# Weight loads on ScalarE's queue, tokens in pairs, and the layer norm's epsilon on GpSimd in a four-layer attention kernel

## The chip, the cores and the metric

The kernel runs on one core of a Trainium2 chip. The core has TensorE (PE in the profile: matmuls, PEld: its weight loads), VectorE (DVE), ScalarE (ACT), GpSimd (POOL) and SyncE (SP), which here only issues DMAs. Each engine works through its own list of instructions in order, and the lists meet at semaphores. The metric is the device time of one execution in microseconds. A profiled execution gives the span and the trace of every instruction.

## The reference

One sequence of 2048 tokens of width 512 in bfloat16 goes through four layers, A, B, A, B, each behind a layer norm and with a residual:

```
def _layernorm(x, axis=-1, eps=1e-5):
    m = jnp.mean(x, axis=axis, keepdims=True)
    v = jnp.var(x, axis=axis, keepdims=True)
    return (x - m) / jnp.sqrt(v + eps)

# A: 32 query heads of 16, one key and one value head
q = (x @ wq) in 32 heads;  k = x @ wk;  v = x @ wv
p = softmax(q k^T * 16 ** -0.5);  out = (p v) @ wo

# B: linear attention, 32 heads of 16
phi(t) = where(t > 0, t + 1, exp(t)) + 1e-6
kv = phi(k)^T v;  z = sum of phi(k);  out = (phi(q) kv / (phi(q) z + 1e-6)) @ wo

x = x + A(_layernorm(x)); x = x + B(_layernorm(x))
x = x + A(_layernorm(x)); x = x + B(_layernorm(x))
```

Both A layers use the same weights, and both B layers.

## The kernel before

**Tiles.** The tokens are 16 tiles of 128 (`x_sb`, resident in SBUF). An A layer first normalises each tile, transposes it, and projects queries (`QT`), keys (`KM`, with a masked copy each for two halves of the heads) and values (`V`). The scores are 2048 blocks of 128 keys by 512 (128 tokens of four heads), by QK matmuls of line 841. A block is made into weights in one of two ways:

- ScalarE takes two or three blocks at once with one exponential out of PSUM (line 1016, tile `PT`).
- VectorE builds an approximate exponential from the bits of an integer (line 1103, tile `FB`), and makes shifted copies of four such blocks together (line 1145, SBUF to SBUF); all versions, weighted by `VW`, go into the value product.

The value product is line 895. VectorE takes blocks only when the keys of all 16 tiles are there.

**Layer norm** (`ln_tile`, lines 676 to 719). For each tile: statistics (`bn_stats`, line 685) and aggregate (line 686) on VectorE, variance plus epsilon (`ve`, line 687) on VectorE, the power -0.5 (`rs`, line 689) on GpSimd, and the normalised tile `xn` (line 692) on VectorE. Then a transpose: in the first layer on PE for tiles 0 to 3 (line 712, with a copy out of PSUM at line 603) and by a DMA from SP for tiles 4 to 15 (line 617). While an A layer's scores still run, finished tiles already pass through the layer norm of the next layer.

**What sets the order.** Nothing is ordered by hand. `Planner` plays the kernel through with a duration and a latency that the code gives each operation, chooses by priority among those that are ready, and, where an operation may run on ACT or DVE (`flex`), by which is free. The resulting lists per engine are what is emitted, with semaphore waits from the dependences. So a changed duration or engine anywhere can redraw the order everywhere. Where PE would stand still, the planner gives it filling matmuls without use (line 827 before and between the layers, line 940 within an A layer).

**The start.** All loads are issued by SP through `dma` (line 540), in order of their priority: tiles 0 to 3 singly, then wk, wv, wq, then tiles 4 to 15 in three blocks of four tiles. The late weights (wo, wqkv, the second wo) follow when all keys of the first layer are planned. POOL runs some thirty small memsets and selects (lines 563 to 595: dummies' operands, identities, masks, `kmask`, the ones column of `va`), DVE eight little ones of `kmask` (line 575). ACT loads its table of functions as its first instruction (line 1674), warms it up with an exponential of one column (line 596), and makes `wkr`, wk repeated eight times, with four copies (line 581). In the first layer, `a_tile` lets no tile but the first enter the layer norm before the first tile's power is done.

Of the kernel before, what the change touches and what calls it, by code (L numbers as in the profile page):

```python
# [10 lines left out]
ALU = mybir.AluOpType  # L11
# [4 lines left out]
P = 128  # L16
# [19 lines left out]
class Planner:  # L36
# [256 lines left out]
    def finalize(self):  # L293
# [15 lines left out]
        dmas = [o for o in self.order[SP] if o.isdma]  # L309
# [103 lines left out]
AHEAD = 20  # L413
CHT = 19
# [6 lines left out]
def bass_interleave_layers__grouped_kv_mqa__linear_attn_block__prompt_kernel(  # L421
# [117 lines left out]
    def dma(dst, src, writes, prio, lat):  # L539
        return op({SP: (0.07, lambda e: e.dma_start(dst, src))}, writes=writes, prio=prio, lat=lat, dma=True)  # L540

    for t in range(4):
        dma(x_sb[:, t, :], xv[:, t, :], [("x", t)], 0.1 * t, 2.5 + 0.5 * t)
    dma(wk[:], A_wk.rearrange("(ft f) c -> f ft c", f=P), ["wk"], 1.0, 4.0)
    dma(wv[:], A_wv.rearrange("(ft f) c -> f ft c", f=P), ["wv"], 1.1, 4.2)
    dma(wq[:], A_wq.rearrange("(ft f) c -> f ft c", f=P), ["wq"], 1.2, 5.5)
    for b in range(1, 4):
        dma(x_sb[:, 4 * b:4 * b + 4, :], xv[:, 4 * b:4 * b + 4, :], [("x", t) for t in range(4 * b, 4 * b + 4)], 2.0 + 0.1 * b, 6.0 + 1.5 * b)
    def late():
        yield ("flag", ("K", 0, T - 1))  # L550
        dma(wo[:], A_wo.rearrange("(g r) c -> r g c", r=P), ["wo"], 3.0, 12.0)
        dma(wqkv[:], B_wqkv.rearrange("(ft f) c -> f ft c", f=P), ["wqkv"], 3.1, 15.0)
        dma(wo2[:], B_wo.rearrange("(g r) c -> r g c", r=P), ["wo2"], 3.2, 16.0)
# [6 lines left out]
    def pool_op(fn, writes, reads=(), dur=0.2, prio=0.0):  # L560
        return op({PO: (dur, fn)}, reads=reads, writes=writes, prio=prio)
# [9 lines left out]
    pool_op(lambda e: e.memset(kmask[:, 0:1], 0.0), ["kmask"], dur=0.1)  # L571
    pool_op(lambda e: e.memset(kmask[:, 1:2], KSC), ["kmask"], dur=0.1)
    for j in range(4):
        for r, v in ((0, KSC), (1, 0.0)):
            op({DV: (0.1, lambda e, j=j, r=r, v=v: e.memset(kmask[32 * j:32 * j + 16, r:r + 1], v))}, writes=["kmask"], prio=0.0)
# [4 lines left out]
    for ft in range(FT):  # L580
        op({AC: (0.17, lambda e, ft=ft: e.copy(
            wkr[:, ft, :].rearrange("p (r d) -> p r d", r=8),
            wk[:, ft, :].unsqueeze(1).to_broadcast([P, 8, DH])))}, reads=["wk"], writes=["wkr"], prio=0.5)
    for i in range(NSH):
# [9 lines left out]
    pool_op(lambda e: e.memset(va[:].rearrange("p t (h c) -> p (t h) c", c=17)[:, :, DH:DH + 1], 1.0),  # L594
            [("va", i) for i in range(8)], dur=2.3, prio=2.6)
    op({AC: (1.6, lambda e: e.activation(warm[:], warm[:], ACTF.Exp))}, writes=["warm"], prio=0.0)
# [19 lines left out]
    def dmat(dst, src, reads, writes, prio):  # L616
        return op({SP: (0.1, lambda e: e.dma_start(dst, src, transpose=True))}, reads=reads, writes=writes, prio=prio, lat=DTL, dma=True)
# [61 lines left out]
    def ln_tile(t, prio, far=False, crit=False):  # L679
# [3 lines left out]
        else:  # L683
# [3 lines left out]
        op({DV: (0.07, lambda e: e.tensor_scalar(out=ve[:, t:t + 1], in0=mv[:, t, 1:2], scalar1=1e-5, scalar2=None, op0=ALU.add))},  # L687
           reads=[("mv", t)], writes=[("ve", t)], prio=prio, lat=0.16)
# [32 lines left out]
    def a_tile(L, t, prio):  # L721
        yield ("flag", ("x", L - 1, t))
        if L == 0 and t:
            yield ("sleep", 0.0)
            yield from until(("rs", 0))
        cr = t in MCRIT[L - 1] if L else False
# [946 lines left out]
    def scalar(e):  # L1673
        e.add_instruction(mybir.InstLoadActFuncSet(name=nc.get_next_instruction_name(), engine=mybir.EngineType.Activation, act_func_set_id=LNEXP))
        pl.emit(AC, e)

    with nc.Block() as block:
# [3 lines left out]
        block.scalar(lambda e: scalar(e))  # L1681
# [29 lines left out]
```

## Time and profile before

| what | value |
|---|---|
| runs | 1515.29, 1515.67, 1517.45 us; median 1515.67 |
| profiled execution: time, span | 1518.41 us, 1516.5 us |
| busy PE, DVE, ACT, POOL | 1460.4, 1437.6, 1474.5, 72.3 us |
| granted PE clock, mean | 0.999 |
| first exponential of scores (ACT) | 15.02 us |
| first block on DVE (line 1103) | 43.48 us |
| tile 0, wk, wv, wq issued by SP at | 0.80, 2.66, 3.14, 3.69 us |
| `ve` on DVE, `rs` on POOL (64 each, mean) | 143 ns, 817 ns |

Busy time is the sum of an engine's instructions without overlaps; a group's mean is of one instruction's own duration, and neighbours on DVE and ACT overlap, so that the step from one start to the next is shorter than the duration. "Idle before" names what released an engine from a wait. The landing of a DMA is the time at which its semaphore is complete.

### The profile page before, as it was taken

To read this page: it belongs to the slowest core of one execution; us is meant where nothing else is said; L and a number is where in the kernel's file an instruction comes from. 1 tells how busy PE (TensorE), PEld (TensorE's weight loads), DVE (VectorE), ACT (ScalarE), POOL (GpSimd) and SP (SyncE) were. 2 spreads that over 40 slices of the span, in tenths; PEclk is the share of its full clock that TensorE was granted. 3 is DMA by queue.
4 is the path that set the end of the run, shared out by engine and by line. 5 is a ranking of instruction groups with operands and counts; after the bars stand their busy time and mean duration, and the time that the engine had idled before them with its cause. 6 is when DMAs were issued, how large, how long until landed. Compare 5 with 4: busy or idle time off the path is not lost.

```text
span 1516.5 us, 36545 instructions
## 1 busy us (share of the span) xinstructions
PE 1460.4 (96%) x14867; PEld 527.4 (35%) x14867; DVE 1437.6 (95%) x2701; ACT 1474.5 (97%) x1502; POOL 72.3 (5%) x126
## 2 busy tenths in 40 slices
PE   7999999999999999999999999999999999999999
PEld 4433333332333333323744323333333333333335
DVE  7899999999999999999866899999999999999996
ACT  7999999999999999999699999999999999999996
POOL 4000000000000000000111000000000000000001
PEclk9999999999999999999999999999999999999999
DMA  4200000000000000000001000000000000000001
GB/s 111 73 5 8 9 10 7 8 5 8 8 9 8 5 8 5 1 2 2 2 16 22 9 8 15 9 8 5 8 9 5 9 8 9 5 5 2 2 2 57
DMA packets 46965, 19.15 MB, mean 13 GB/s; under 512 B 40656, under 2 KB 46288, under 8 KB 46800
## 3 DMA queue, kind: packets, MB, share of 16 engines
q1 hardware_dynamic: 46800, 16.82, 4.8%
q8 instruction: 119, 1.95, 0.6%
q14 instruction: 46, 0.38, 0.1%
HBM read 5.28 MB, written 2.10 MB: 5 GB/s over the span
## 4 chain that ended last, share of the span: by engine, by line
issue 79%; PE 11%; ACT 5%; POOL 2%; DVE 1%; DMA 1%; SPq 0%; POOLq 0%; ACTq 0%
ACT PT L1016 5%; PE ps L895 2%; POOL rs L689 2%; PE ps L609 2%; PE ps L841 2%; PE ps L766 1%; PE ps L827 1%; PE ps L940 1%; DMA wq<-in_A_wq_dram 0%; PE ps L1439 0%; PE ps L660 0%; DMA xnT<-xn 0%; PE ps L1187 0%; SPq L540 0%; POOL VW L736 0%
## 5 line engine op out<-in xcount | busy, mean ns | idle before, releaser
L1016 ACT ACTIVATE PT<-ps 128x1024 bf16<-128x1024 f32 (+1 forms) x1338 | 1408.3, 1198 | 6.8 <-PE ps L841 5.1
L1103 DVE TENSOR_SCALAR FB<-ps 128x512 int16<-128x512 f32 x1042 | 685.5, 682 | 8.0 <-PE ps L841 5.8
L841 PE MATMUL ps<-QT,KM 32*128 32x512 bf16 x4096 | 538.4, 385 | 20.8 <-ACT PT L1016 15.4
L895 PE MATMUL ps<-FB,VW 128*32 128x512 bf16 x4168 | 543.6, 385 | 12.9 <-ACT PT L1016 6.4
L1145 DVE TENSOR_SCALAR FB<-FB 128x2048 int16<-128x2048 int16 x786 | 516.2, 677 | 0.7
L895 PE MATMUL ps<-PT,V 128*32 128x512 bf16 x3054 | 488.7, 387 | 7.2 <-ACT PT L1016 5.3
L841 PEld LDWEIGHTS ps<-QT,KM 32*128 32x128 bf16 x4096 | 134.9, 91 | 400.8 <-ACT PT L1016 249.1
L895 PEld LDWEIGHTS ps<-FB,VW 128*32 128x32 bf16 x4168 | 134.3, 94 | 185.8 <-issue 88.4
L940 PE MATMUL ps<-QT,V 128*32 128x512 bf16 (+6 forms) x798 | 197.4, 319 | 1.3 <-DVE QT L1275 0.8
L895 PEld LDWEIGHTS ps<-PT,V 128*32 128x32 bf16 x3054 | 118.8, 93 | 124.1 <-issue 62.5
L689 POOL TENSOR_TENSOR rs<-ve,mhalf 128x1 f32<-128x1 f32 x64 | 52.2, 817 | 1337.7 <-DVE ve L687 1328.5
L940 PEld LDWEIGHTS ps<-QT,V 128*32 128x32 bf16 x798 | 63.8, 95 | 91.1 <-issue 62.4
L609 PE MATMUL ps<-wqkv,xnT 128*128 128x512 bf16 (+1 forms) x272 | 84.8, 373 | 0.5 <-DMA xnT<-xn 0.3
L1187 PE MATMUL ps<-identF,sacc 128*128 128x128 f32 x256 | 47.7, 292 | 2.4 <-DVE sacc L1168 2.0
L1272 ACT ACTIVATE phE<-ps 128x512 bf16<-128x512 f32 (+1 forms) x66 | 41.6, 631 | 7.8 <-PE ps L766 5.8
L1168 DVE COPY sacc<-ps 128x512 f32<-128x512 f32 x64 | 43.7, 682 | 4.9 <-PE ps L895 4.9
L685 DVE BATCH_NORM_STATS2 st<-x_sb 128x6 f32<-128x512 bf16 x60 | 40.7, 679 | 3.2 <-DMA x_sb<-in_A_x_dram 3.0
L609 PE MATMUL ps<-wo,OT 128*128 128x512 bf16 x120 | 42.0, 387 | 0.9 <-DMA OT<-Osb 0.8
L766 PE MATMUL ps<-xnT,wq 128*128 128x128 bf16 x480 | 39.7, 223 | 0.6 <-DMA wq<-in_A_wq_dram 0.5
L766 PE MATMUL ps<-xnT,wqkv 128*128 128x128 bf16 x512 | 39.6, 220 | 0.2
L609 PEld LDWEIGHTS ps<-wqkv,xnT 128*128 128x128 bf16 x272 | 22.2, 97 | 49.4 <-issue 32.8
L1187 PEld LDWEIGHTS ps<-identF,sacc 128*128 128x128 f32 x256 | 27.4, 140 | 25.7 <-issue 14.4
(142 smaller groups left out, 645.0 us busy)
## 6 DMA issues: line engine op xcount, KB each, us to landing
out_dram<-x_sb SPq DMA_DIRECT2D x16, 128.0 KB, 1.7
x_sb<-in_A_x_dram SPq DMA_DIRECT2D x3, 512.0 KB, 6.8
wqkv<-in_B_wqkv_dram SPq DMA_DIRECT2D x1, 1536.0 KB, 8.8
xnT<-xn SPq DMA_TRANSPOSE x48, 2.4
x_sb<-in_A_x_dram SPq DMA_DIRECT2D x4, 128.0 KB, 2.3
wq<-in_A_wq_dram SPq DMA_DIRECT2D x1, 512.0 KB, 4.9
wo<-in_A_wo_dram SPq DMA_DIRECT2D x1, 512.0 KB, 4.1
wo<-in_B_wo_dram SPq DMA_DIRECT2D x1, 512.0 KB, 9.6
```

Of the source, the lines that this page charges most:

```text
L609: return e.matmul(dst, lhsT=l, rhs=r, start=(k == 0), stop=(k == len(pairs) - 1))
L689: op({PO: (0.55, lambda e: e.tensor_tensor(out=rs[:, t:t + 1], in0=ve[:, t:t + 1], in1=mhalf[:], op=ALU.pow))}, reads=[("ve", t), "mhalf"] ...
L766: ins = e.matmul(dst[:, g * P:(g + 1) * P], lhsT=lhs(g, k), rhs=rhs(k), start=(k == 0), stop=(k == FT - 1))
L841: return e.matmul(bank(b), lhsT=KM[r, sg.par, kt * P:(kt + 1) * P], rhs=QT[r, sg.t, :], start=True, stop=True)
L895: ins = e.matmul(ps[32 * j:32 * j + 32, ACC * 512:(ACC + 1) * 512], lhsT=V[:, kt, :] if w is None else VW[:, kt, w, :], rhs=ap, start=(k = ...
L940: o = op({PE: (n / 2400.0, lambda e: e.matmul(ps[32 * j:32 * j + 32, b * 512:b * 512 + n], lhsT=V0[:], rhs=QT[:, sg.t, 0:n], start=st, sto ...
L1016: ex = op({AC: (0.051 + 0.4267 * n, lambda e, n=n, s_=s_, p_=p_: e.activation(PT[:, p_, 0:n * 512], ps[:, s_ * 512:(s_ + n) * 512], ACTF.E ...
L1103: o = op({DV: (0.602, lambda e: e.tensor_scalar(out=dst.bitcast(I16), in0=bank(b), scalar1=VB, scalar2=VLO, op0=ALU.add, op1=ALU.max))}, w ...
L1145: o = op({en: (du, lambda e, w=w, g_=g_: e.tensor_scalar(out=FB[:, g_, 0:n].bitcast(I16), in0=FB[:, f_, 0:n].bitcast(I16), scalar1=float(w ...
L1168: o = op({DV: (0.6, lambda e, src=src: e.tensor_copy(src, bank(ACC)))}, writes=[B_(ACC), key], prio=0.0, lat=0.15)
L1187: o = op({PE: (0.12, lambda e, c=c: e.transpose(ps[:, b * 512 + c * P:b * 512 + (c + 1) * P], src[:, c * P:(c + 1) * P], identF[:]))}, rea ...
L1272: op({AC: (0.07 + n / 1200.0, lambda e: e.activation(phE[:, i, 0:n], bank(b, n), ACTF.Exp))}, reads=[B_(b)], writes=[("phE", i)], prio=pr ...
```

## The change

- wk, wv and wq are issued by ACT's queue, as its first three instructions; the table load and the warming exponential come behind them (both now in `first`).
- Tiles 4 to 15 are loaded in six pairs, by SP.
- Epsilon is added on POOL rather than DVE, with a priority ahead of POOL's other work.
- POOL's two memsets of `kmask` come first, and the ones column of `va` moves behind the last key of the first layer.
- In the first layer, tiles from the third on enter the layer norm only when the second tile's power is done as well.
- The planner's durations and latencies of the loads, the DMA transposes, the `wkr` copies, the small memsets and the table load are given other values. `POWD` is not used anywhere.

```diff
-        dmas = [o for o in self.order[SP] if o.isdma]
+        dmas = [o for e in (AC, SP) for o in self.order[e] if o.isdma]
...
-    def dma(dst, src, writes, prio, lat):
-        return op({SP: (0.07, lambda e: e.dma_start(dst, src))}, writes=writes, prio=prio, lat=lat, dma=True)
+    def dma(dst, src, writes, prio, lat, eng=SP, dur=0.52):
+        return op({eng: (dur, lambda e: e.dma_start(dst, src))}, writes=writes, prio=prio, lat=lat, dma=True)
 
     for t in range(4):
-        dma(x_sb[:, t, :], xv[:, t, :], [("x", t)], 0.1 * t, 2.5 + 0.5 * t)
-    dma(wk[:], A_wk.rearrange("(ft f) c -> f ft c", f=P), ["wk"], 1.0, 4.0)
-    dma(wv[:], A_wv.rearrange("(ft f) c -> f ft c", f=P), ["wv"], 1.1, 4.2)
-    dma(wq[:], A_wq.rearrange("(ft f) c -> f ft c", f=P), ["wq"], 1.2, 5.5)
-    for b in range(1, 4):
-        dma(x_sb[:, 4 * b:4 * b + 4, :], xv[:, 4 * b:4 * b + 4, :], [("x", t) for t in range(4 * b, 4 * b + 4)], 2.0 + 0.1 * b, 6.0 + 1.5 * b)
+        dma(x_sb[:, t, :], xv[:, t, :], [("x", t)], 0.1 * t, 1.7 + 0.15 * t, dur=0.46 if t else 1.26)
+    dma(wk[:], A_wk.rearrange("(ft f) c -> f ft c", f=P), ["wk"], -9.0, 1.9, AC, 1.3)
+    dma(wv[:], A_wv.rearrange("(ft f) c -> f ft c", f=P), ["wv"], -8.0, 2.4, AC)
+    dma(wq[:], A_wq.rearrange("(ft f) c -> f ft c", f=P), ["wq"], -7.0, 4.2, AC)
+    for b in range(2, 8):
+        dma(x_sb[:, 2 * b:2 * b + 2, :], xv[:, 2 * b:2 * b + 2, :], [("x", t) for t in range(2 * b, 2 * b + 2)], 2.0 + 0.1 * b, 3.2 + 0.35 * b)
+
     def late():
         yield ("flag", ("K", 0, T - 1))
+        pool_op(lambda e: e.memset(va[:].rearrange("p t (h c) -> p (t h) c", c=17)[:, :, DH:DH + 1], 1.0), [("va", i) for i in range(8)], dur=1.2, prio=5.0)
...
-    pool_op(lambda e: e.memset(kmask[:, 0:1], 0.0), ["kmask"], dur=0.1)
-    pool_op(lambda e: e.memset(kmask[:, 1:2], KSC), ["kmask"], dur=0.1)
+    pool_op(lambda e: e.memset(kmask[:, 0:1], 0.0), ["kmask"], dur=0.95, prio=-2.0)
+    pool_op(lambda e: e.memset(kmask[:, 1:2], KSC), ["kmask"], dur=0.1, prio=-2.0)
...
-    op({AC: (1.6, lambda e: e.activation(warm[:], warm[:], ACTF.Exp))}, writes=["warm"], prio=0.0)
+
+    def first(e):
+        e.add_instruction(mybir.InstLoadActFuncSet(name=nc.get_next_instruction_name(), engine=mybir.EngineType.Activation, act_func_set_id=LNEXP))
+        return e.activation(warm[:], warm[:], ACTF.Exp)
+
+    op({AC: (1.48, first)}, writes=["warm"], prio=-6.0)
...
-        return op({SP: (0.1, lambda e: e.dma_start(dst, src, transpose=True))}, reads=reads, writes=writes, prio=prio, lat=DTL, dma=True)
+        return op({SP: (0.5, lambda e: e.dma_start(dst, src, transpose=True))}, reads=reads, writes=writes, prio=prio, lat=DTL - 0.4, dma=True)
...
-        op({DV: (0.07, lambda e: e.tensor_scalar(out=ve[:, t:t + 1], in0=mv[:, t, 1:2], scalar1=1e-5, scalar2=None, op0=ALU.add))},
-           reads=[("mv", t)], writes=[("ve", t)], prio=prio, lat=0.16)
+        op({PO: (0.12, lambda e: e.tensor_scalar(out=ve[:, t:t + 1], in0=mv[:, t, 1:2], scalar1=1e-5, scalar2=None, op0=ALU.add))},
+           reads=[("mv", t)], writes=[("ve", t)], prio=prio - 9.0)
...
             yield from until(("rs", 0))
+            if t > 1:
+                yield ("sleep", 0.0)
+                yield from until(("rs", 1))
...
-        block.scalar(lambda e: scalar(e))
+        block.scalar(lambda e: pl.emit(AC, e))
```

In the built order of the changed kernel PE has 14820 matmuls (14865 before), DVE 2644 instructions (2703), ACT 1507 (1504), POOL 194 (130) and SP 103 (103).

More of the change, by code (lines that the diff above doesn't have):

```diff
@@ L413 @@
 AHEAD = 20
+POWD = 0.6
 CHT = 19
@@ L580, in bass_interleave_layers__grouped_kv_mqa__linear_attn_block__prompt_kernel @@
     for ft in range(FT):
-        op({AC: (0.17, lambda e, ft=ft: e.copy(
+        op({AC: (0.26, lambda e, ft=ft: e.copy(
             wkr[:, ft, :].rearrange("p (r d) -> p r d", r=8),
```

13 lines of the change are left out of this document (4 added, 9 removed).

## The prediction

> **What bounds the kernel now.** I read the page first (its busy shares and its costliest groups), then a table of stretches, the timeline of the first 24 us, and the timeline of one layer norm inside a full stretch.
>
> The page, the groups that fill ScalarE (ACT) and VectorE (DVE), and the one on GpSimd (POOL) that the change touches:
>
> ```profile
> PE 1460.4 (96%) x14867; PEld 527.4 (35%) x14867; DVE 1437.6 (95%) x2701; ACT 1474.5 (97%) x1502; POOL 72.3 (5%) x126
> ...
> L1016 ACT ACTIVATE PT<-ps 128x1024 bf16<-128x1024 f32 (+1 forms) x1338 | 1408.3, 1198 | 6.8 <-PE ps L841 5.1
> L1103 DVE TENSOR_SCALAR FB<-ps 128x512 int16<-128x512 f32 x1042 | 685.5, 682 | 8.0 <-PE ps L841 5.8
> ...
> L689 POOL TENSOR_TENSOR rs<-ve,mhalf 128x1 f32<-128x1 f32 x64 | 52.2, 817 | 1337.7 <-DVE ve L687 1328.5
> ```
>
> The table of stretches: the head, then the two attention stretches. Columns are busy microseconds of each engine.
>
> ```profile
> 0.00:15.00 15.00, 8.98 (x86) 7.21 (x87) 8.09 (x35) 5.90 (x14) 7.72 (x34) 1.00 0.62 177
> ...
> 100.00:700.00 600.00, 582.65 (x5831) 188.64 (x5830) 595.53 (x1071) 597.78 (x587) 17.53 (x15) 1.00 0.03 7
> 860.00:1440.00 580.00, 561.74 (x5707) 187.74 (x5703) 574.52 (x1045) 577.05 (x579) 15.20 (x14) 1.00 0.03 7
> ```
>
> In the attention stretches three engines are full together: ACT idles 2.2 and 3.0 us, DVE 4.5 and 5.5. They share 4096 score blocks (3054 on ACT, 1042 on DVE). So time is gained by starting that stream earlier or by giving ACT and DVE less to do, and lost by any new stop of either. The head leaves ACT idle for 9.1 of 15 us.
>
> Timeline of the head (start, duration, engine, line, operation, idle before it):
>
> ```profile
> 4.12 0.15 DVE L687 TENSOR_SCALAR ve<-mv 128x1 f32<-128x1 f32 x1
> 4.36 0.55 POOL L689 TENSOR_TENSOR rs<-ve,mhalf 128x1 f32<-128x1 f32 x1
> 4.87 0.37 POOL L590 TENSOR_SCALAR_AFFINE_SELECT mask<-mask 128x136 bf16<-128x136 bf16 x1
> ...
> 8.61 1.89 PE L766 MATMUL ps<-xnT,wq 128*128 128x128 bf16 x16 [0.52 <-DMA wq<-in_A_wq_dram]
> 10.08 0.69 DVE L685 BATCH_NORM_STATS2 st<-x_sb 128x6 f32<-128x512 bf16 x1 [2.63 <-DMA x_sb<-in_A_x_dram]
> 10.42 2.53 PE L827 MATMUL ps<-zz,V 128*32 128x128 bf16 x22
> 10.69 0.20 DVE L687 TENSOR_SCALAR ve<-mv 128x1 f32<-128x1 f32 x2
> ...
> 12.88 0.68 PE L712 MATMUL ps<-ident,xn 128*128 128x128 bf16 x8
> ...
> 15.02 1.02 ACT L1016 ACTIVATE PT<-ps 128x1024 bf16<-128x1024 f32 x1 [0.38 <-PE ps L841]
> ...
> 16.61 7.81 ACT L1016 ACTIVATE PT<-ps 128x1024 bf16<-128x1024 f32 x7
> ```
>
> DVE stands at 7.4 us with tiles 2 and 3 normalised but for their epsilon, because the next instruction in its order is the statistics of tile 4, whose 512 KB land at 10.05. Epsilon of tiles 2 and 3, their powers, the transposes on PE at 12.88 and the first exponential at 15.02 follow from that. The exponentials run without a break from 16.61.
>
> One layer norm inside a full stretch (DVE, then POOL):
>
> ```profile
> 1415.10 0.14 DVE L687 TENSOR_SCALAR ve<-mv 128x1 f32<-128x1 f32 x1
> 1415.16 1.28 DVE L1145 TENSOR_SCALAR FB<-FB 128x2048 int16<-128x2048 int16 x2
> 1416.89 0.41 DVE L692 TENSOR_SCALAR xn<-x_sb,mv,rs 128x512 bf16<-128x512 bf16 x1 [0.44 <-POOL rs L689]
> ...
> 1415.32 1.53 POOL L689 TENSOR_TENSOR rs<-ve,mhalf 128x1 f32<-128x1 f32 x1 [42.42 <-DVE ve L687]
> ```
>
> The power takes 0.55 us where DVE does something else, but 0.93 to 1.53 beside the shifted copies L1145: it gets through only at their ends. L1145 itself keeps its step of 0.60 us. The reader is to see that epsilon costs DVE only a step of 0.06 us (1415.10 to 1415.16), not its 0.14.
>
> **The change part by part.** The profiled execution has a span of 1516.5 and a time of 1518.41; the runs' median is 1515.67, 2.74 lower. The sum is a difference against the profiled span, and I put it on the median.
>
> Queues. SP loses the issues of wk, wv, wq (2.66 to 4.24, 1.58 us) and issues six pairs where it had three blocks (0.51 each, so +1.6): its last token issue ends near 5.9 as now, but tiles 4 and 5 are issued at 2.66, not 4.24. ACT gains three issues (0.8 to about 2.4) ahead of the table load (1.28) and the warming exponential (0.20): done near 4.0. That is hidden: ACT's next work, the wkr copies, now starts at 5.00 because wk lands at 4.98, and it would then land near 3.1. Were the issues 1 us each, wkr would end 0.6 late and tile 0's copy on ACT with it.
>
> Memsets. kmask first lets DVE do its eight small memsets (0.10 apart) from 1.1 to 2.0, before tile 0 lands at 2.93; three of them now sit between the steps of tile 0 (about 0.1 us gained). The va memset (1.17 on POOL) goes behind the keys, where POOL is idle: nothing.
>
> Epsilon of tile 0. On POOL one mask select (0.37) comes between epsilon and power. Epsilon on POOL isn't in the trace; bounds are 0.10 (a 128x1 memset) and 0.55 (the power, same shape). I take 0.15, as it is one simple operation. Statistics end 3.64, aggregate 3.88, epsilon 4.11, select 4.48, power 5.03, xn at 5.07 (now 4.95).
>
> First exponential. Transposes to 6.15, twelve dummy matmuls to 7.5, V and K to 8.15, sixteen Q matmuls (1.89) to 10.05 with no wait for wq, tile 1's transposes, now directly behind, to 10.4, fourteen dummies in place of 22 (0.115 each) to 12.0, then 0.43 to the first exponential: 12.45 against 15.02. It has three blocks, not two. Then a key copy (0.37), the query copy of tile 1 (0.59) and an unbroken stream from about 14.9 with three blocks done, against 16.61 with two: 1.7 plus one block (1464 ns for three, 0.49), about 2.1 gained. Bounds: 2.9 if the stream never breaks, 0.6 if the small weight descriptors delay tiles 0 and 1 by 0.5 (wv lands 1.03 after wk), epsilon takes 0.55 and PE follows. **-2.1.**
>
> The rest of the order. The planner redraws it all. Counting both built orders: ACT has 20 more two-bank exponentials (0.982 each by form) and 14 fewer of three banks (1.464), -0.9; two query copies (0.63), one further xnT copy (0.61), two va copies (0.65) and a 512-wide key copy (0.90) fewer, one OT (0.64) and one small key copy (0.37) more: -3.9 in all. DVE gets two blocks more, six full shifts more and nine short ones fewer (+1.9 net), query, va, xnT, OT and key copies (+3.3), and loses 64 steps of 0.06 (-3.8): +1.4. PE's filling matmuls go from 798 to 754. Between -3.9 and +1.4 I stay near ACT, which idles least: **-3.0.**
>
> Epsilon in the two middle passages (700 to 860), where DVE waits for the power: aggregate to power is 0.27 now (739.48 to 739.75), and 0.08 + 0.15 + 0.07 on POOL: **+0.3**; with epsilon at 0.55, ten waits of 0.4 more, +4; at 0.10, nothing.
>
> The new wait. In 30 layer norms of the full stretches DVE now does aggregate, one or more operations, epsilon, then two or more, then xn. In the new order twelve have only two L1145 between aggregate and xn, so xn stands 1.2 us behind. Epsilon on POOL must get past the first or second copy (done about 1.25), then the power needs 0.55: xn at about 1.85, a stop of 0.65. Six more lose about 0.1. Together 8.4 us of DVE against 1.9 now (0.44 four times and two of 0.07): +6.5. Behind xn on DVE wait score blocks, and behind them PE's score matmuls and ACT. Bounds for the span: 0, if DVE's other idle time (10.0 less 1.9 in the two stretches) takes it in, and +6.5 if all is passed on. After the stop at 1416.89 ACT's starts 1418.86 and 1420.03 lie 1.17 apart, where two-bank groups without a stop start 0.90 apart (657.22, 658.12, 659.02): something over half arrives at ACT at once; but late DVE work then waits less for PE. I take a quarter, **+1.6.**
>
> A rule against this change: the Trainium skill, SBUF — State Buffer, section SBUF: two separate sides, says that GpSimd and VectorE's two-port modes lock their common port for a whole instruction, whichever comes first. The trace shows one side of that: power waits, L1145 keeps its step. By the rule epsilon would also hold DVE, 30 times 0.15 by my value, and at a quarter the sum would be 1.1 higher.
>
> Sum: -2.1 - 3.0 + 0.3 + 1.6 = -3.2, so 1515.67 - 3.2 = 1512.5.
>
> **The rivals.** *The waits are absorbed.* DVE waits for others for 8 us in the full stretches, and ACT's load falls by the full 3.9: -2.1 - 3.9 = -6.0, 1509.7. Against it: ACT's late starts behind a stop.
>
> *Slower: DVE becomes the bound, by xn waiting for the power.* The place is the twelve pairs of L1145 before xn. -2.1 + 1.4 + 0.3 + 6.5 = +6.1, 1521.8. It decides once DVE rather than ACT sets the end of each stretch and more than half of the 6.5 us is passed on (-2.1 + 1.4 + 0.3 + 3.4 = +3.0). For it: the 0.44 us stops exist already. Against: only six in 30 now.
>
> *The queues bring nothing.* The DMA share is 1.06 to 1.11 between 6 and 11 us, so tokens and wq share full engines, and weights issued at 0.8 delay tiles 0 to 3. Head -0.6: -0.6 - 3.0 + 0.3 + 1.6 = -1.7, 1514.0. Against: 1.58 us of issue is really saved, and the share is 0.59 to 0.64 from 4 to 6. The Trainium skill, DMA: Bandwidth & Descriptors, section Issuing engines are not separate DMA queues, says the same: only issue time is saved.
>
> **How the numbers follow.** A difference of 0.2% (3.0 us) is about what a measurement here can tell from none. Forecast 0.42 (own range 1510 to 1515; faster 0.27, same 0.15); absorbed 0.22 (faster 0.20, same 0.02); slower 0.21 (slower 0.19, same 0.02); queues 0.15 (same 0.11, faster 0.02, slower 0.02). Together 0.49, 0.30, 0.21. Range 1507 to 1520: to the absorbed case with the head at -2.9 and past most of the slower one.
>
> **What would show it.** Right: first exponential near 12.5 and no break after 15; no 2.6 us stop of DVE in the head; epsilon on POOL about 0.15 alone; stops of about 0.65 before xn behind two L1145; ACT's exponentials 0.9 us shorter in sum. Wrong: tile 0 landing after 3.4; epsilon of 0.5 us; DVE's idle before xn above 10 us together with a longer ACT group; new idle time between 700 and 860, whose order I can't price.

## The result and the profile after

The changed kernel takes 1521.5 us (median; 1520.6 to 1526.12) against 1515.67 (1515.29 to 1517.66). The ratio is 1.0040, with a 95% interval of 1.0028 to 1.0051: it is slower by 0.4%, where 1512.5 was forecast (range 1507 to 1520). The profiled execution has a time of 1521.09 and a span of 1519.3.

The groups of the changed kernel that answer to those shown of before (line, engine, operation, tiles, shape, count | busy us, mean ns of one | idle us just before them and what ended it). L1025 is the exponential, L1112 VectorE's block, L693 epsilon, L695 the power, L698 the normalised tile:

```profile
L1025 ACT ACTIVATE PT<-ps 128x1024 bf16<-128x1024 f32 (+1 forms) x1344 | 1409.0, 1191 | 13.3 <-PE ps L850 10.5 <-PE ps L904 0.7
L1112 DVE TENSOR_SCALAR FB<-ps 128x512 int16<-128x512 f32 x1044 | 687.6, 683 | 5.3 <-PE ps L850 4.3
L695 POOL TENSOR_TENSOR rs<-ve,mhalf 128x1 f32<-128x1 f32 x64 | 37.2, 583 | 4.3
L693 POOL TENSOR_SCALAR ve<-mv 128x1 f32<-128x1 f32 x64 | 32.1, 505 | 1335.1 <-DVE mv L692 1328.4 <-DVE V L609 6.6
L698 DVE TENSOR_SCALAR xn<-x_sb,mv,rs 128x512 bf16<-128x512 bf16 x64 | 25.9, 412 | 14.8 <-POOL rs L695 14.3
```

ScalarE (ACT) is no less busy with exponentials (1409.0 us; 1408.3 before) and stands twice as long before them (13.3; 6.8). VectorE stands 14.8 us before xn. Epsilon has a mean of 505 ns, where 150 was taken.

The same stretches as before (window; length; busy us of PE, PEld, DVE, ACT, POOL with counts; granted clock; DMA share; GB/s):

```profile
0.00:15.00 15.00, 9.18 (x97) 7.47 (x98) 8.10 (x29) 7.06 (x15) 7.73 (x39) 1.00 0.61 178
...
100.00:700.00 600.00, 567.86 (x5728) 184.26 (x5777) 593.32 (x1058) 595.89 (x585) 22.06 (x30) 1.00 0.03 7
860.00:1440.00 580.00, 547.93 (x5636) 185.16 (x5669) 573.00 (x1028) 574.96 (x581) 19.52 (x28) 1.00 0.04 7
```

In the two attention stretches ACT now idles 4.1 and 5.0 us (2.2 and 3.0 before) and VectorE 6.7 and 7.0 (4.5 and 5.5). PE's busy time misses some records and isn't compared.

The head of the changed kernel (start, duration, engine, line, operation, idle before it):

```profile
4.21 0.23 POOL L693 TENSOR_SCALAR ve<-mv 128x1 f32<-128x1 f32 x1 [0.99 <-DVE mv L692]
4.72 0.57 POOL L695 TENSOR_TENSOR rs<-ve,mhalf 128x1 f32<-128x1 f32 x1
...
8.26 1.91 PE L775 MATMUL ps<-xnT,wq 128*128 128x128 bf16 x16
...
11.13 1.25 DVE L691 BATCH_NORM_STATS2 st<-x_sb 128x6 f32<-128x512 bf16 x2
...
12.58 1.45 ACT L1025 ACTIVATE PT<-ps 128x1536 bf16<-128x1536 f32 x1 [1.78 <-PE ps L850]
...
14.64 3.73 ACT L1025 ACTIVATE PT<-ps 128x1536 bf16<-128x1536 f32 x3
```

The queries no longer wait for wq, VectorE's statistics no longer wait for a token block, the first exponential starts at 12.58 with three blocks and the stream is unbroken from 14.64. The head does what was forecast, for the reasons given; how far its size can be relied on is said below.

One layer norm inside a full stretch (DVE, then POOL):

```profile
1408.70 0.17 DVE L692 BATCH_NORM_AGGREGATE mv<-st 128x2 f32<-128x6 f32 x1
1408.79 1.26 DVE L1154 TENSOR_SCALAR FB<-FB 128x2048 int16<-128x2048 int16 x2
1410.78 0.41 DVE L698 TENSOR_SCALAR xn<-x_sb,mv,rs 128x512 bf16<-128x512 bf16 x1 [0.73 <-POOL rs L695]
...
1408.96 1.13 POOL L693 TENSOR_SCALAR ve<-mv 128x1 f32<-128x1 f32 x1 [38.72 <-DVE mv L692]
1410.17 0.57 POOL L695 TENSOR_TENSOR rs<-ve,mhalf 128x1 f32<-128x1 f32 x1
```

Epsilon is done only when both shifted copies are through, and the power begins after that. VectorE stands for 0.73 us. Twelve layer norms of the two stretches show this stop of 0.72 to 0.73; all stops before xn there sum to 9.13 us, against 1.92 before.

**Where the time went.** From the traces one can read when the n-th of the 4096 score blocks had been turned into weights. The first trace of the kernel before has its clock granted at 0.50 from 30.1 to 33.5 us (0.89 over 30 to 45), so a second trace of it (below) is the base: span 1513.9, time 1515.86, near the median.

| up to block | before, second trace | changed kernel | difference |
|---|---|---|---|
| 200 (head) | 90.17 | 88.11 | -2.05 |
| 2048 (end of layer 1's scores) | 718.44 | 719.05 | +0.61 |
| 2300 (after the passage) | 855.61 | 859.02 | +3.41 |
| 4096 | 1474.90 | 1480.43 | +5.54 |
| end of span | 1513.90 | 1519.35 | +5.45 |

The head gained 2.05 us in these two traces. 2.66 went in the first stretch, 2.80 between blocks 2048 and 2300, and 2.13 after that.

### The profile page after: what moved, and what is told of

Same layout as the page of the kernel before. It is cut to its first block, busy times and chain, and to the rows that moved or that the text cites. A ratio compares the mean times of both kernels' runs of the same rounds, so it can differ in the third digit from the quotient of the medians.

```text
span 1519.3 us, 36361 instructions
## 1 busy us (share of the span) xinstructions
PE 1431.7 (94%) x14707; PEld 521.8 (34%) x14822; DVE 1435.6 (94%) x2642; ACT 1473.3 (97%) x1502; POOL 89.1 (6%) x190
## 5 line engine op out<-in xcount | busy, mean ns | idle before, releaser
L1025 ACT ACTIVATE PT<-ps 128x1024 bf16<-128x1024 f32 (+1 forms) x1344 | 1409.0, 1191 | 13.3 <-PE ps L850 10.5
L1112 DVE TENSOR_SCALAR FB<-ps 128x512 int16<-128x512 f32 x1044 | 687.6, 683 | 5.3 <-PE ps L850 4.3
L904 PE MATMUL ps<-FB,VW 128*32 128x512 bf16 x4176 | 527.7, 385 | 16.5 <-DVE sacc L1177 6.9
L904 PE MATMUL ps<-PT,V 128*32 128x512 bf16 x3052 | 474.9, 387 | 11.5 <-ACT PT L1025 6.5
L904 PEld LDWEIGHTS ps<-FB,VW 128*32 128x32 bf16 x4176 | 129.5, 94 | 188.5 <-issue 96.2
L949 PE MATMUL ps<-QT,V 128*32 128x512 bf16 (+5 forms) x754 | 190.6, 324 | 3.7 <-DVE FB L1112 3.4
L904 PEld LDWEIGHTS ps<-PT,V 128*32 128x32 bf16 x3052 | 115.1, 93 | 129.7 <-issue 63.5
L693 POOL TENSOR_SCALAR ve<-mv 128x1 f32<-128x1 f32 x64 | 32.1, 505 | 1335.1 <-DVE mv L692 1328.4
L615 PE MATMUL ps<-wqkv,xnT 128*128 128x512 bf16 (+1 forms) x210 | 67.5, 369 | 4.3 <-issue 2.5
L698 DVE TENSOR_SCALAR xn<-x_sb,mv,rs 128x512 bf16<-128x512 bf16 x64 | 25.9, 412 | 14.8 <-POOL rs L695 14.3
L695 POOL TENSOR_TENSOR rs<-ve,mhalf 128x1 f32<-128x1 f32 x64 | 37.2, 583 | 4.3
```

The costliest lines, as they stand in the source:

```text
L615: return e.matmul(dst, lhsT=l, rhs=r, start=(k == 0), stop=(k == len(pairs) - 1))
L904: ins = e.matmul(ps[32 * j:32 * j + 32, ACC * 512:(ACC + 1) * 512], lhsT=V[:, kt, :] if w is None else VW[:, kt, w, :], rhs=ap, start=(k = ...
L949: o = op({PE: (n / 2400.0, lambda e: e.matmul(ps[32 * j:32 * j + 32, b * 512:b * 512 + n], lhsT=V0[:], rhs=QT[:, sg.t, 0:n], start=st, sto ...
L1025: ex = op({AC: (0.051 + 0.4267 * n, lambda e, n=n, s_=s_, p_=p_: e.activation(PT[:, p_, 0:n * 512], ps[:, s_ * 512:(s_ + n) * 512], ACTF.E ...
L1112: o = op({DV: (0.602, lambda e: e.tensor_scalar(out=dst.bitcast(I16), in0=bank(b), scalar1=VB, scalar2=VLO, op0=ALU.add, op1=ALU.max))}, w ...
```

## The experiments

The theory at the start: the 9.1 us in which VectorE stands before xn are handed on to the stream, and that is the loss. The rivals: the newly drawn order is worse for other reasons and the stops fall into time that VectorE would idle anyway; the other edits lose it; or epsilon costs on GpSimd (POOL) wherever it stands. Each ratio below is to runs of the kernel before on the same chip; medians in microseconds come from several chips, so differences between kernels are better taken from the ratios. The granted clock dips in part of the executions (last section); where that bears on a comparison, it is said. Where a kernel keeps an order "as it was", the planner runs unchanged and the lists are edited after it.

**The stops taken away.** xn moved back in VectorE's list, all else kept (`lns` collects the five operations of each layer norm):

```
+    for n, (t, ag, vo, pw, xo) in enumerate(lns):
+        dv = pl.order[DV]
+        if not (16 <= n < 31 or 48 <= n < 63):
+            continue
+        i = dv.index(xo)
+        got = sum(o.opts[DV][0] for o in dv[dv.index(ag) + 1:i])
+        while got < 1.85 and xo not in dv[i + 1].deps:
+            got += dv[i + 1].opts[DV][0]
+            dv[i], dv[i + 1] = dv[i + 1], dv[i]
+            i += 1
     pl.finalize()
```

> The changed kernel with every list as it was, but in the two full stretches each xn stands behind enough of VectorE's following operations (1.85 us of them between aggregate and xn, by the planner's durations) that the power is done: 18 of the 30 xn move by one or two operations. Nothing else moves. Theory of the stops (the loss is the 9.1 us that VectorE stands before xn in the two stretches, 1.9 before the change, passed on to the stream): these stops go, and 4 to 7 us with them: 1515 to 1517.5. Rival, the drawn order (the new order of blocks and copies is the worse one, and the stops fall into time that VectorE would idle anyway): 1520.5 to 1522.5, with the idle time named after other releasers.

Measured: 1515.4 us, ratio 0.9994 (0.9985 to 1.0002). Groups and stretches of this kernel:

```profile
L1114 DVE TENSOR_SCALAR FB<-ps 128x512 int16<-128x512 f32 x1044 | 686.4, 680 | 7.9 <-PE ps L852 6.1
...
L699 DVE TENSOR_SCALAR xn<-x_sb,mv,rs 128x512 bf16<-128x512 bf16 x64 | 25.8, 411 | 5.8 <-POOL rs L696 5.5
```

```profile
100.00:700.00 600.00, 582.42 (x5808) 185.46 (x5806) 596.94 (x1064) 598.17 (x588) 23.23 (x30) 1.00 0.03 7
860.00:1440.00 580.00, 560.31 (x5701) 186.22 (x5697) 575.92 (x1033) 576.49 (x584) 20.39 (x28) 1.00 0.04 7
```

Moving nothing but xn (20 of the 30, by the trace) gives back 6.1 us by the medians, 7.0 by the ratios, and 5.5 by the two stretches of the traces (next run). ACT's idle time falls from 4.1 to 1.8 and from 5.0 to 3.5. But of the 9 us less before xn, 2.6 come back as waits before VectorE's own blocks (5.3 to 7.9): there VectorE was early and now waits for a score matmul again.

**Half of it.** The same, in the first stretch alone (`if not 16 <= n < 31`).

> As the run with xn moved back, but in the first full stretch alone; the second keeps its 3.9 us of stops. The first stretch took 3.4 us less there, the second 2.1. Both theories of the stops: 3.4 us below the changed kernel, about 1517.7 (1516.5 to 1519). Rival, the moves work only together or the gain was in the passage: no more than 1 or at least 5 us below it.

Measured: 1518.15 us, ratio 1.0006 (0.9994 to 1.0017). From block 200 to 2048 it takes 627.55 us, as with both stretches moved (627.57; changed kernel 630.94); from 2300 to 4096 621.42, as the changed kernel (621.41; both moved 619.30). So the stops cost 3.4 us in the first stretch and 2.1 in the second, each by itself.

**More stops.** Each xn moved forward, behind one operation after its aggregate:

```
+        i, a = dv.index(xo), dv.index(ag)
+        while i > a + 2 and dv[i - 1] not in xo.deps:
+            dv[i], dv[i - 1] = dv[i - 1], dv[i]
+            i -= 1
```

> The changed kernel with every list as it was, but each xn of the two full stretches stands behind only one operation after its aggregate. By the changed kernel's trace epsilon then passes behind that one shifted copy (0.57 us), the power follows (0.57), and VectorE stands 0.73 us before nearly every one of the 30: about 21 us of stops instead of 9.1. Theory that a stop is paid only beyond the waits for score matmuls (4.2 us of them left in the changed kernel's two stretches, as against 6.7 without stops): the waits are used up, nearly the whole of the 12 us more is paid: 1529.5 to 1533.5. Rival, two thirds of each stop are paid: 1528 to 1530. Rival, the stops don't set the time: 1522 or less.

Measured: 1538.79 us, ratio 1.0141 (1.0126 to 1.0155), above every expectation. A layer norm of it (DVE, then POOL), and its groups:

```profile
1385.65 0.17 DVE L693 BATCH_NORM_AGGREGATE mv<-st 128x2 f32<-128x6 f32 x1
1385.74 0.66 DVE L1156 TENSOR_SCALAR FB<-FB 128x2048 int16<-128x2048 int16 x1
1387.17 0.41 DVE L699 TENSOR_SCALAR xn<-x_sb,mv,rs 128x512 bf16<-128x512 bf16 x1 [0.77 <-POOL rs L696]
...
1385.91 0.57 POOL L694 TENSOR_SCALAR ve<-mv 128x1 f32<-128x1 f32 x1 [44.17 <-DVE mv L693]
1386.56 0.57 POOL L696 TENSOR_TENSOR rs<-ve,mhalf 128x1 f32<-128x1 f32 x1
```

```profile
L1114 DVE TENSOR_SCALAR FB<-ps 128x512 int16<-128x512 f32 x1044 | 685.5, 680 | 8.8 <-PE ps L852 7.6
...
L699 DVE TENSOR_SCALAR xn<-x_sb,mv,rs 128x512 bf16<-128x512 bf16 x64 | 26.1, 415 | 27.8 <-POOL rs L696 27.6
```

The stops are 22.2 us, 13.1 more than in the changed kernel. The time is 15.3 us longer by the ratios (about 12.5 to 18 by their intervals) and 17.3 by the medians, and the stretches of the trace account for it: 638.88 us from block 200 to 2048 (+7.9) and 631.44 from 2300 to 4096 (+10.0). So about all of the stops is paid, and the two thirds of the rival (8.7 us) are out. The trace alone shows more than all, but each of its two stretches holds one dip of the clock, which the changed kernel's have not (the granted clock is the third figure from the end):

```profile
531.60:535.00 3.40, 3.40 (x26) 1.05 (x18) 2.65 (x6) 1.34 (x2) 0.00 (x0) 0.51 0.13 27
985.50:988.90 3.40, 3.40 (x25) 1.13 (x22) 2.39 (x6) 3.25 (x3) 0.00 (x0) 0.50 0.00 0
```

Such a dip cost about 1.4 us in the passage (last section). These two begin 1.8 and 3.0 us after the xn of such a stop (at 529.76 and 982.47), and between the two PE stands still for 1.32 and 2.07 us. Whether a stop brings on a dip wasn't tested; the changed kernel's stretches have three PE pauses of 0.95 to 1.14 us, two of them behind such stops, and no dip. Waits for score matmuls went up as well (4.2 to 6.5 us).

**Epsilon back on VectorE, newly planned**, with everything else of the change:

```
-        op({PO: (0.12, lambda e: e.tensor_scalar(out=ve[:, t:t + 1], ...
-           reads=[("mv", t)], writes=[("ve", t)], prio=prio - 9.0)
+        op({DV: (0.07, lambda e: e.tensor_scalar(out=ve[:, t:t + 1], ...
+           reads=[("mv", t)], writes=[("ve", t)], prio=prio, lat=0.16)
```

> The changed kernel with epsilon alone back on VectorE, everything else of the change kept; the planner draws a new order. Theory of the stops: the head's gain of about 4 us (time of the 200th score block, after minus before) stays, the stops of xn fall back to about 2 us: 1511.5 (1510 to 1513.5). Rival, the other edits lose it behind the head (the transposes' and loads' new planner values, the weights on ScalarE's queue): above 1517. Rival, any newly drawn order is off by several us: nothing to be said, 1510 to 1522.

Measured: 1512.32 us, ratio 0.9971 (0.9959 to 0.9982): faster than both kernels, with 0.5 us of stops in the stretches. The number is inside the range, but not by the head's gain of 4 us that was expected: block 200 comes at 89.45, only 0.7 us before the second trace of the kernel before. The stretches make up the rest (626.73 and 617.78 us against 628.28 and 619.29). The queues, pairs, memsets and new planner values don't lose the time by themselves.

**Epsilon alone on GpSimd, newly planned**: that replacement the other way round, in the kernel before.

> The kernel before with epsilon alone moved to GpSimd; the planner draws a new order. No gain in the head. In this order only four layer norms of the two stretches have exactly two shifted copies and nothing else between aggregate and xn (14 in the changed kernel). Theory of the stops, at 0.73 us for each such pair and 0.1 for one copy: about 3.5 us of stops against 1.9, and 64 steps of 0.06 us less on VectorE: 1515.5 (1513.5 to 1517.5). Rival, epsilon on GpSimd costs wherever it stands: 1519 or more.

Measured: 1513.4 us, ratio 0.9983 (0.9974 to 0.9993), also faster, and a little below the range. Epsilon on GpSimd doesn't cost wherever it stands: here the stops are 3.7 us, and only three of them are over 0.7. What I had not expected is its head: with the old queues the first exponential starts at 12.52, as early as in the changed kernel's own trace (other traces of that kernel's head have 11.10 to 11.28, last section).

**The stops of that kernel taken away**, by the first edit:

> The kernel before with epsilon alone on GpSimd, in the order that it had, but with each xn of the two full stretches moved back by one to three operations of VectorE's list where less than 1.85 us lay between aggregate and xn. That kernel had 3.7 us of stops there and stood 2.7 us below the kernel before. Theory of the stops, at the price found in the changed kernel (9.1 us of stops gone, 6.1 us gained, two thirds): 2.4 us more, so about 5 us below the kernel before (4 to 6.5). Rival, what was gained there came of the moved list and not of the stops: no change, 1.5 to 3.5 us below the kernel before.

Measured: 1514.06 us, ratio 0.9974 (0.9964 to 0.9984), 3.9 us below the kernel before where 5 were expected; the interval overlaps that of the run without the move. Both traces, with the moved kernel second:

```profile
L1103 DVE TENSOR_SCALAR FB<-ps 128x512 int16<-128x512 f32 x1035 | 679.0, 680 | 6.2 <-PE ps L841 4.5
...
L692 DVE TENSOR_SCALAR xn<-x_sb,mv,rs 128x512 bf16<-128x512 bf16 x64 | 26.0, 407 | 10.2 <-POOL rs L689 9.9
```

```profile
L1105 DVE TENSOR_SCALAR FB<-ps 128x512 int16<-128x512 f32 x1035 | 681.1, 682 | 8.6 <-PE ps L843 6.3
...
L693 DVE TENSOR_SCALAR xn<-x_sb,mv,rs 128x512 bf16<-128x512 bf16 x64 | 25.8, 405 | 6.7 <-POOL rs L690 6.5
```

Of 3.5 us less before xn, 2.4 come back before the blocks. From VectorE's first block to block 2048 it takes 676.51 and 676.59 us, from block 2300 to 4096 it takes 618.42 and 618.86 (a dip of the clock lies in the latter, at 1036): nothing is gained that can be measured. So a stop isn't paid at a fixed share, and the theory in its first form (two thirds) falls. VectorE's idle time of both stretches, added up from the traces (from 60 us, and from 12 us after VectorE's first block of the third layer, each to its last block of the stretch), shows how it is paid:

| kernel | before xn | before its blocks, for score matmuls | all of VectorE | ACT |
|---|---|---|---|---|
| before, second trace | 1.9 | 7.4 | 10.3 | 5.1 |
| epsilon alone on GpSimd | 3.7 | 5.3 | 10.4 | 5.3 |
| the same, xn moved back | 0.2 | 7.7 | 10.0 | 5.6 |
| changed kernel | 9.1 | 4.2 | 14.2 | 9.4 |
| the same, xn moved back | 0.2 | 6.7 | 7.9 | 5.8 |
| the same, xn moved forward | 22.2 | 6.5 | 30.9 | 23.0 |

Without stops VectorE waits for score matmuls about 7 us. Stops take the place of some 2.5 us of these waits, in both orders, and no more than that in any kernel of the table; what lies above makes VectorE's idle time longer, and with it ACT's.

**Epsilon moved without a new order**, in both directions: in the changed kernel, from GpSimd to VectorE right behind the aggregate; in the kernel before, from VectorE to GpSimd right before the power.

```
+        pl.order[PO].remove(vo)
+        vo.eng = DV
+        pl.order[DV].insert(pl.order[DV].index(ag) + 1, vo)
```

```
+        pl.order[DV].remove(vo)
+        vo.eng = PO
+        pl.order[PO].insert(pl.order[PO].index(pw), vo)
```

> The changed kernel with every list as it was, but epsilon taken from GpSimd's list and put on VectorE right behind its aggregate; no new order is drawn. Theory of the stops: the power then begins within the first shifted copy, and the stop behind two copies is 0.44 us as in the kernel before instead of 0.73: 14 times 0.29 is 4.1 us less, and 64 steps of 0.06 are 3.8 more, 1.8 of them in the full stretches: 1519.5 (1518 to 1521). Rival, the drawn order: VectorE's added steps alone count, 1521.5 to 1524.

Measured: 1520.84 us, ratio 1.0032 (1.0022 to 1.0043), inside the range, but not by the sum expected. All seven executions had a mean granted clock below 1 (0.993 to 0.998), of the 24 of the kernel before beside them 17 had 1.000, so part of the ratio may be that. A layer norm of it (DVE):

```profile
1407.19 0.17 DVE L693 BATCH_NORM_AGGREGATE mv<-st 128x2 f32<-128x6 f32 x1
1407.39 0.15 DVE L694 TENSOR_SCALAR ve<-mv 128x1 f32<-128x1 f32 x1
1407.46 1.28 DVE L1156 TENSOR_SCALAR FB<-FB 128x2048 int16<-128x2048 int16 x2
1408.82 0.41 DVE L699 TENSOR_SCALAR xn<-x_sb,mv,rs 128x512 bf16<-128x512 bf16 x1
```

The stops nearly go: 0.08 us behind two copies (1408.74 to 1408.82), and 1.0 us in the two stretches instead of 9.1, where 0.44 was expected behind each pair of copies (fourteen pairs were taken, the changed kernel's trace shows twelve). But epsilon right behind its own aggregate costs VectorE more than a step of 0.06: from the aggregate's start to that of the copies it is 0.27 us, and 0.09 in the changed kernel (1408.70 to 1408.79). That is 0.18 in each of 30 layer norms, 5.4 us of VectorE's time. In the kernel before another operation stands between the two. Not all of it is seen in the time: the stretches take 628.47 and 621.72 us, with xn moved back 627.57 and 619.30, and in the 621.72 lies a dip (at 971.5).

> The kernel before with every list as it was, but epsilon taken from VectorE's list and put into GpSimd's right before its power; no new order is drawn. Here 19 of the 30 layer norms of the two stretches have three operations or more between aggregate and xn. Theory of the stops: 2 to 4 us of them against 1.9, under the waits for score matmuls (7.4 us in the two stretches), so not paid; VectorE saves 64 steps of 0.06; the first exponential comes 0.5 to 1.5 us earlier, as epsilon of the third and fourth tile no longer stands behind the statistics of the fifth: 1513 to 1515.5, against 1515.7. Rival, epsilon on GpSimd costs as such: 1517 or more.

Measured: 1517.74 us, ratio 1.0001 (0.9993 to 1.0010): no difference. From VectorE's first block of a layer to the layer's last block it takes 677.17 and 628.54 us, in the second trace of the kernel before 677.32 and 628.84. So 64 steps fewer on VectorE, 3.8 us, bring 0.5: with 1.2 us of stops (all 30 layer norms have three operations or more between aggregate and xn, by the trace), VectorE's load doesn't set the stretch. The expected gain in the head wasn't there either (first exponential 14.08; 14.01 in the second trace of before): xn of the third and fourth tile still stand behind the fifth's statistics in this order.

**The planner told what epsilon takes**, 1.13 us in place of 0.12, everywhere or only in the layer norms beside the full stretches:

```
-        op({PO: (0.12, lambda e: e.tensor_scalar(out=ve[:, t:t + 1], ...
+        op({PO: (1.13, lambda e: e.tensor_scalar(out=ve[:, t:t + 1], ...
```

```
+        op({PO: (1.13 if prio > 4.9 else 0.12, lambda e: ...
```

> The changed kernel, epsilon still on GpSimd, but the planner is told that it takes 1.13 us (the time behind two shifted copies in the changed kernel's trace) instead of 0.12, so that it puts xn later; it draws a new order. In that order every layer norm of the two full stretches has three operations or more between aggregate and xn, or two and a small one. Theory of the stops: under 1 us of stops in the stretches, the head as in the changed kernel, 64 steps of VectorE saved: 1509.5 to 1513. Rival, epsilon's place on GpSimd costs something else than the stops: 1515 or more.

Measured: 1524.51 us, ratio 1.0045 (1.0031 to 1.0058), far off and not measurably different from the changed kernel (1.0040). The stops in the stretches are gone as expected (0.07 us), and from block 200 to 2048 it takes 627.61 us (628.27 in the second trace of before). It loses elsewhere: 3.4 us between blocks 2048 and 2600 (244.90; 241.47), 2.7 in the tail after the last block (41.67; 39.00). Between the stretches the planner now puts xn late although epsilon takes 0.22 there: from aggregate to xn 17 layer norms take 36.6 us together, 23.2 in the changed kernel. In the tail xn follows its aggregate as before (1.21 us), so why that is longer is open. Its trace also has a long dip of the clock, which lies in the head:

```profile
30.00:45.00 15.00, 13.66 (x112) 5.24 (x112) 9.01 (x22) 12.39 (x12) 7.26 (x19) 0.63 0.59 163
```

> The changed kernel, with the planner told 1.13 us for epsilon only in the layer norms that run beside the full stretches (tiles 0 to 13 of the second and fourth layer), and 0.12 elsewhere as in the changed kernel. The order is drawn anew. What was lost with 1.13 us told everywhere (the passage to the third layer about 10 us longer, the tail 2.7) should not come back. Theory of the stops: 1511 to 1515.5, with about 1 us of stops left. Rival, epsilon on GpSimd costs outside the stretches too: 1517 or more.

Measured: 1514.5 us (1513.7 to 1515.09), ratio 0.9977 (0.9967 to 0.9986), as expected, with 1.3 us of stops. The same edits as the changed kernel, epsilon on GpSimd, and one planner value: 0.6% faster than with 0.12 by the ratios.

**What a newly drawn order does by itself.** The planner's duration of a token tile's statistics, 0.6, was given as 0.61 or 0.62 in the kernel before, and as 0.61 in the changed kernel:

```
-            op({DV: (0.6, lambda e: e.bn_stats(
+            op({DV: (0.61, lambda e: e.bn_stats(
```

> The kernel before with the same unrelated planner value changed (0.61 us instead of 0.60): another order, epsilon on VectorE, the old head. Measures what a newly drawn order alone does. Theory of the stops: no more than 2 us either way, 1514 to 1518. Rival, drawn orders differ by as much as the change did: 1519 or more, or 1512 or less.

> As the run before, with 0.62 us: a third order of the kernel before. Theory of the stops: 1514 to 1518. Rival, drawn orders differ by as much as the change did: 1519 or more, or 1512 or less.

Measured: 1518.8 us, ratio 1.0009 (0.9999 to 1.0019), and 1518.14, ratio 1.0001 (0.9992 to 1.0010). Both lie above their range in microseconds, but the kernel before beside them takes 1517.56, 1.9 us above the median that the range started from. Two other orders of the kernel before are not measurably different from it.

> The changed kernel with one planner value changed that has nothing to do with it (a token tile's statistics 0.61 us instead of 0.60), so that another order is drawn. Five layer norms of the two stretches now have exactly two shifted copies between aggregate and xn, where the changed kernel has fourteen. Theory of the stops: about 4.5 us of stops instead of 9.1, and the time follows: 1516 to 1518.5. Rival, the stops do not matter and the order is good or bad for other reasons: no relation, 1512 to 1524.

Measured: 1521.24 us, ratio 1.0023 (1.0012 to 1.0033): still slower, less so than the changed kernel, with 4.2 us of stops instead of 9.1.

> The other drawn order of the changed kernel (statistics given as 0.61 us, 4.2 us of stops in the two stretches, 3.5 us above the kernel before), with xn moved back in the same way. Theory of the stops: 2.8 us gained, about 0.7 us above the kernel before (-0.5 to 1.8). Rival: no gain, 2.5 to 4.5 above it.

Measured: 1522.55 us, ratio 1.0030 (1.0020 to 1.0040): a miss, no gain in the medians from 4.2 us of stops taken away. Part of that is the 2.5 us that waits for matmuls take in. Part can be the clock: nine of these ten executions had a mean granted clock below 1, of the kernel before's beside them 12 of 21. The one at 1.000 took 1517.78 us (the kernel before at 1.000: 1515.38 to 1517.35), and without the move the three at 1.000 took 1518.84 to 1519.42 (the kernel before: 1515.24 to 1517.56). So a gain of 1 to 1.5 us isn't excluded, and how slow this order is beside its stops and dips is open.

**The kernel before, traced a second time.**

> The kernel before as it is, for a second trace of it, as the first one has its clock granted at 0.89 between 30 and 45 us and a time 2.7 us above the median. All theories: 1515 to 1518, and without that dip VectorE's first block earlier than 43.48, by 1 to 2.5 us.

Measured: 1515.86 us, VectorE's first block at 41.12 instead of 43.48. Its group before xn and its stretches are those of the first trace:

```profile
L692 DVE TENSOR_SCALAR xn<-x_sb,mv,rs 128x512 bf16<-128x512 bf16 x64 | 26.1, 412 | 8.2 <-POOL rs L689 8.0
...
100.00:700.00 600.00, 571.45 (x5776) 188.19 (x5822) 595.65 (x1073) 597.81 (x587) 17.16 (x15) 1.00 0.04 7
860.00:1440.00 580.00, 552.79 (x5674) 188.00 (x5714) 574.57 (x1046) 577.09 (x579) 15.58 (x14) 1.00 0.03 7
```

## Why the prediction was wrong, step by step

| step | forecast | measured |
|---|---|---|
| head | -2.1 | -2.05 at block 200 (-3.5 in two other traces of the same head) |
| the new wait before xn | +1.6 | +5.5 (3.4 and 2.1 in the two stretches) |
| rest of the order, with epsilon in the passages | -3.0 + 0.3 | about +2.0 (5.45 + 2.05 - 5.5) |
| sum | -3.2 | +5.45 (traces); +5.8 (medians) |

- **Head: right in its causes**: no wait for wq, no wait of VectorE for a token block, three blocks at 12.58 (12.45 forecast), no break from 14.64 (14.9). That the size agrees so closely is partly luck of the traces compared: in two other traces of the same head (xn moved back in both stretches, and in one) block 200 comes at 86.64 and 86.70, 3.5 us before the kernel before, beyond the forecast's bound of 2.9. And the queues aren't the only cure of VectorE's stop: epsilon on GpSimd under a new plan, with the old queues, starts the exponentials at 12.52 and has block 200 at 88.34.
- **The new wait: the mechanism was right, the share passed on was not.** "They sum to 8.4 us" was near (9.1), stops of 0.65 are 0.73, and they stand behind two shifted copies as forecast. The step that failed is "I take a quarter, +1.6". I argued that late VectorE work then waits less for PE. It does, but only for some 2.5 us of the two stretches; beyond that a stop was paid nearly in full: 8.9 us more of stops than with xn moved back cost 5.5, and in the kernel with 22 us of stops 13.1 more cost about 15, dips of the clock included. The forecast had those 8 us of waits in view and took them for a cover of unknown strength; the rows to compare were the sum of the stops and the sum of the waits that stops can replace.
- **Epsilon's price** "as one simple operation", 0.15 us, is 0.22 alone. Beside shifted copies it is 0.57 behind one, 1.13 behind two in a row and 1.77 behind three in a row (the timeline below). That it waits for the copy was foreseen ("must get past the first or second copy"); that copies in a row count as one, so that it passes only at the end of the last, was not.
- **Rest of the order: the step "I stay near ACT, -3.0" failed.** ACT's busy time fell by 1.2 us (1474.5 to 1473.3), not by 3.9; its exponentials took 0.7 more, not 0.9 less. Even without the stops, where ACT's load in the same order is 1471.9, the time doesn't follow it. With the stops taken out the kernel is level with the kernel before (0.9994), though its head is ahead, so the rest of its order is about 2 us worse and not 3 better. Two other orders of the kernel before don't differ from it measurably; the changed kernel's other order stays slower with its stops moved (1.0030, with more dips of the clock), while the one planned with 1.13 us for epsilon beside the stretches is faster (0.9977). What makes one order better than another, beside the stops, is open. The 2.8 us between blocks 2048 and 2300 are mostly back by block 2600 (+0.95) and lost again later, so they have no one place.
- **Epsilon in the passages, +0.3: not the loss.** VectorE's waits for the power between the stretches fell, from 5.1 to 2.1 us.
- **The rivals.** The slower one, VectorE as the bound through the new wait (1521.8), named the place, and it is what happened, though its sum is not: it had VectorE's added work (+1.4, where VectorE's busy time fell by 2.0) and all of the wait (+6.5), where the runs show 5.5 for the wait and an unexplained 2. "Absorbed" held for about 2.5 us of stops. "The queues bring nothing" is not told apart by these runs. The head did gain, but as this rival says tiles 0 to 3 land later (3.18, 3.86, 6.21 and 6.99 us; 2.93, 3.46, 4.21 and 4.58 before). With the new queues and epsilon on VectorE block 200 comes 0.7 us earlier, with the old queues and epsilon on GpSimd 1.8. Its row was also read too high: the DMA share from 7 to 8 us is 0.93.
- **The rule of the Trainium skill**, SBUF — State Buffer, section SBUF: two separate sides, gives the shared port to whichever of GpSimd and VectorE comes first. By it epsilon would also have held VectorE, for 1.1 us more in the sum. The trace shows one side only: the shifted copies keep their mean (681 ns; 680 before), and every wait is GpSimd's, also where it began first. Here in the changed kernel a power that takes 0.57 alone begins 0.16 us before a shifted copy, and it is the power that is drawn out (DVE, then POOL):

```profile
163.27 0.68 DVE L1154 TENSOR_SCALAR FB<-FB 128x2048 int16<-128x2048 int16 x1
163.87 1.28 DVE L1112 TENSOR_SCALAR FB<-ps 128x512 int16<-128x512 f32 x2
...
163.11 0.88 POOL L695 TENSOR_TENSOR rs<-ve,mhalf 128x1 f32<-128x1 f32 x1
```

What the forecast said would show it wrong did: VectorE's idle time before xn above 10 us (14.8), with a longer ACT group, and epsilon at 0.5 us in the mean (0.505).

## What to carry to other kernels

A stop of one engine is free only as far as it takes the place of waits that the engine has anyway for its suppliers (here 2.5 of some 7 us): add up both from the trace, and price what lies above that at its full length. A planner that takes 0.12 us for an operation which takes 1.13 beside the work it is planned into puts its users too early each time; the true value given only where it holds took this kernel from a ratio of 1.0040 to 0.9977, and given everywhere it brought nothing (1.0045). Where an instruction is moved to another engine, try it in the old order and in a new one: here the move by itself changed nothing in the kernel before's order (1.0001), and newly drawn orders with epsilon on GpSimd went from 0.9977 to 1.0045.

## What the runs showed of the hardware that was not expected

Epsilon on GpSimd passes only when a run of shifted copies on VectorE ends. Three copies in a row, from the kernel with xn moved back (DVE, then POOL):

```profile
261.12 1.86 DVE L1156 TENSOR_SCALAR FB<-FB 128x2048 int16<-128x2048 int16 x3
...
263.75 0.41 DVE L699 TENSOR_SCALAR xn<-x_sb,mv,rs 128x512 bf16<-128x512 bf16 x1 [0.17 <-POOL rs L696]
...
261.29 1.77 POOL L694 TENSOR_SCALAR ve<-mv 128x1 f32<-128x1 f32 x1 [42.33 <-DVE mv L693]
263.14 0.57 POOL L696 TENSOR_TENSOR rs<-ve,mhalf 128x1 f32<-128x1 f32 x1
```

In part of the executions of most kernels the granted clock falls to 0.50, in the traces for 3.4 us at a time and twice for 13.6, mostly at different places from one execution to the next. Dips of 3.4 us cost about 1.4 each in the passage: from block 2048 to 2600 the changed kernel's order takes 241.81 us without one, 243.17 with one at 780.4 (xn moved back in one stretch), and 244.62 with two, at 780.3 and 797.4 (in both stretches). By the mean granted clock, how many executions have one differs by kernel: none of six with epsilon back on VectorE under a new plan, all seven with epsilon back in the old order; whether the order brings them on is open. In the trace of epsilon moved in the old order a dip of 13.6 us, from 24.0 on, cost 4.2: level with the kernel before at block 20 (24.82; 24.75), 4.25 behind at block 50 (42.56; 38.31), and about as far behind at block 4096:

```profile
15.00:30.00 15.00, 13.81 (x131) 5.72 (x128) 12.66 (x35) 13.53 (x14) 7.68 (x20) 0.80 0.43 72
30.00:45.00 15.00, 14.91 (x137) 6.42 (x136) 9.31 (x25) 12.84 (x12) 5.82 (x15) 0.75 0.45 134
```

The sixteen query matmuls of the first tile took 1.91 us in the changed kernel and 1.33 to 1.59 in three other traces of the same head, with the granted clock shown as 1.00 in all of them. Against the trace with 1.36 the four transposes behind them took 0.63 (0.39 there) and the fourteen filling matmuls 1.68 (0.96 there); the first exponential came at 12.58, in the others at 11.1 to 11.3. The head varies by 1.5 us from this slower PE work alone.
